# An attention and FFN block on one core: the whole program order placed by a list scheduler, row maxima taken over two PSUM banks at once, and the last 512 queries cut into tiles of 128

## The chip, the cores and the metric

The kernel runs on one core of a Trainium2 chip. Five engines work side by side, each with its own instruction queue: TensorE (PE, matrix products, with PEld for its weight loads), VectorE (DVE), ScalarE (ACT), GpSimd (POOL) and SyncE (SP, which issues DMA transfers here). An engine runs its queue in order and waits on semaphores where it needs another engine's result. Products land in PSUM, which has eight banks of 128 x 512 fp32; the other memory is SBUF. The metric is the device time of the whole program in microseconds (us), the median of several runs.

## The reference

The block is a pre-norm transformer layer over 2048 tokens of width 512, with 32 heads of width 16 and an FFN of width 1792.

```python
qkv = (x @ wqkv).reshape(B, S, 3, H, Dh).transpose(2, 0, 3, 1, 4)   # x here is layernorm(A_x)
scores = einsum("bhqd,bhkd->bhqk", q, k) * (Dh ** -0.5)
o = einsum("bhqk,bhkd->bhqd", softmax(scores, axis=-1), v)
h = x + o.transpose(0, 2, 1, 3).reshape(B, S, D) @ wo
h2 = h + (gelu(ln(h) @ w_gate) * (ln(h) @ w_up)) @ w_down           # gelu in its tanh form
```

Each head has 2048 x 2048 scores. The softmax subtracts the true row maximum, so every score is computed twice: once with queries on the partitions to find the maximum of each row, and once transposed, with keys on the partitions, for the exponential.

## The kernel before

**Tiling.** Tokens are 16 tiles of 128 (`NT`), or 4 chunks of 512 (`NCH`). Four heads make a slot (`NSLOT` = 8), and in a slot each head owns one of four 32-row groups of the PE array. A unit is one chunk of queries and one slot; there are 32.

**First pass, the maxima (p1).** For each unit, `p1_pair` (L518) makes two products at a time, 128 queries against 512 keys of two heads, into two of the banks 0 to 2. `p1_consume` (L527) reduces each bank on DVE to one column of `PM`. After 32 pairs, `negm_pre` (L532 to L541) reduces `PM` to the negated maxima `NEGM` on DVE and splits each into three bf16 parts on POOL. `item_negm` (L548) transposes these parts on PE, ACT copies them to `STG`, and four small DMA transfers (L552) write them as three further rows of `QT`. The keys have ones in those rows (`kbias`), so the second product contains score minus maximum.

**Second pass, the exponentials (p2).** `p2_pair` (L568) makes two products of 128 keys against 512 queries, into two of the banks 3 to 5. `p2_consume` (L578) takes the exponential of each bank on ACT into a ring `PT` of 12 slots. `pv_burst` (L589) multiplies eight of them with the values, four heads side by side by column groups, and accumulates in bank 6 (`PVB`). A column of ones beside the values gives the sum of each row. After 64 of them ACT copies the bank to `OA`; `item_ofin` transposes it (L604), ACT copies it to `OAT`, and POOL divides (L612, L615) into `Otok`.

**The rest.** The projections of Q, K and V (`item_projT`, `item_projV`), and for each finished chunk the output projection, the second layer norm, gate, up and down (`item_onT` to `item_down`), are cut into pieces in one stream, `Dense`. While the two passes run it owns bank 7 alone, and ACT empties it. In the FFN, POOL does the elementwise work of gelu around a tanh on ACT (`gelu_chain`, L729 to L735). When `tail_mode` is set, after the last exponential, ACT uses a gelu of its own and DVE helps.

**What sets the order.** `Plan` records each engine's instructions in the order in which the Python code calls it, and turns the reads and writes given into semaphore waits; nothing is reordered later. The main loop (L817) goes by ticks. A tick has one pair of first-pass products and one pair of second-pass products, in one group:

```python
P.group_begin("pe")
t1 = p1_pair(tick // 32, tick % 32, gp1, signal_last=not p2_ok) if p1_ok else []
t2l = p2_pair(t2 // 32, t2 % 32, 1 - gp1) if p2_ok else []
P.group_end("pe")
```

`group_end` collects all waits of the four products and puts them ahead of the first. The second pass runs 42 ticks behind the first (`P2_START` = 32 + `LAGX`). After the group a tick has a piece of the dense stream, a burst of eight PV products, or up to two `dummy` products (L810), whose results nobody reads. The head before the loop loads x, the QKV weights and wo in six transfers (L294 to L297), normalises all 16 token tiles and transposes them, and makes five projections before the first tick. The three FFN weights (`qkv_finished`) are loaded into the place of the QKV weights once all projections are made.

## Time and profile before

| | us |
|---|---|
| median of 3 runs | 1482.26 (1481.47 to 1482.4) |
| span of the profiled execution | 1477.5 |
| what lies around the profiled span (median less span) | 4.8 |
| busy: PE, DVE, ACT, POOL | 1102.5, 1301.6, 1290.3, 458.3 |
| share of the span: PE, DVE, ACT, POOL | 75%, 88%, 87%, 31% |
| mean granted TensorE clock | 0.991 of full speed |

The span runs from the first to the last instruction; the run's time includes what lies around it. In the profile a row of a group gives the line, the engine, the operation with its tiles (written from read), the shapes, how many there were, their busy time and mean duration (ns), and the idle time ahead of them with the instruction that ended most of it. Busy times of overlapping instructions are counted once, so the busy time of a group can be less than count times mean. Chains of waits and timelines name the same lines. A row of the waits gives who waited for whom, the total, the number of times and the longest. In the view of stretches each engine's busy time is followed by its number of instructions.

### The profile page before, as it was taken

The page shows a single profiled execution, that of the slowest core. Times are in us where ns is not written, and L with a number is a line of the kernel's source. Part 1 is how long each engine was busy: PE and PEld are TensorE (multiplying, and loading weights), DVE is VectorE, ACT ScalarE, POOL GpSimd, SP SyncE. Part 2 cuts the span into 40 slices and gives each one's busy share as a digit, 9 for nine tenths or more (in the row PEclk, how much of TensorE's full clock was granted, in tenths as well). Part 3 has the DMA queues.
Part 4 walks back from the last instruction along what each step waited for, and adds up shares of the span by engine and source line. Part 5 has one row for each costly group of instructions (what it writes and reads, how often), then busy time and mean ns, then how long its engine had stood idle before and what let it go on. Part 6 is the DMA issues. An engine that isn't in the chain of part 4 may idle for free.

```text
span 1477.5 us, 24601 instructions
## 1 busy us (share of the span) xinstructions
PE 1102.5 (75%) x8353; PEld 304.0 (21%) x8494; DVE 1301.6 (88%) x2159; ACT 1290.3 (87%) x2473; POOL 458.3 (31%) x593
## 2 busy tenths in 40 slices
PE   4977777776777777777887777777877777777869
PEld 2311111111112211111222211111222211111224
DVE  5989999998999999999999999999999999998023
ACT  3459999997999999999999999999999999999941
POOL 6000011110112245555212345554112345555130
PEclk9999999998999999999999999999999999999989
DMA  3000000013000000000000000000000000000000
GB/s 114 1 1 2 1 2 2 1 40 112 1 16 1 1 2 2 1 1 2 4 14 14 2 1 2 1 1 1 7 25 1 2 1 2 2 1 2 8 22 16
DMA packets 11531, 15.88 MB, mean 11 GB/s; under 512 B 1040, under 2 KB 9872, under 8 KB 11408
## 3 DMA queue, kind: packets, MB, share of 16 engines
q1 hardware_dynamic: 11408, 14.29, 2.9%
q8 instruction: 71, 1.16, 0.3%
q14 instruction: 52, 0.43, 0.1%
HBM read 11.80 MB, written 2.10 MB: 9 GB/s over the span
## 4 chain that ended last, share of the span: by engine, by line
ACT 32%; DVE 31%; PE 19%; issue 16%; POOL 1%; DMA 1%; SPq 0%; POOLq 0%; ACTq 0%
DVE PM L527 30%; ACT PT L578 27%; PE pbank L518 12%; PE pbank L794 2%; PE pbank L568 1%; PE pbank L462 1%; PE pbank L751 1%; ACT OA L440 1%; PE pbank L770 1%; ACT u_sb L440 1%; DVE stats L315 1%; ACT g_sb L440 1%; ACT sqj L682 0%; ACT OnT L440 0%; ACT QT L440 0%
## 5 line engine op out<-in xcount | busy, mean ns | idle before, releaser
L527 DVE TENSOR_REDUCE PM<-pbank 128x1 f32<-128x512 f32 x2048 | 1258.3, 683 | 70.7 <-PE pbank L568 56.2
L578 ACT ACTIVATE PT<-pbank 128x512 bf16<-128x512 f32 x2048 | 1117.8, 603 | 81.8 <-PE pbank L568 10.3
L518 PE MATMUL pbank<-KT,QT 32*128 32x512 bf16 x2048 | 399.5, 384 | 311.9 <-DVE PM L527 162.3
L568 PE MATMUL pbank<-QT,KT 32*128 32x512 bf16 x2048 | 398.1, 386 | 4.6 <-ACT PT L578 4.3
L518 PEld LDWEIGHTS pbank<-KT,QT 32*128 32x128 bf16 x2048 | 105.0, 91 | 776.3 <-DVE PM L527 767.6
L810 PE MATMUL pbank<-ones_bf,ident 128*128 128x512 bf16 x756 | 239.9, 386 | 5.0 <-ACT PT L578 3.5
L612 POOL TENSOR_TENSOR LINV<-OAT,negone 128x16 f32<-128x16 f32 x32 | 93.2, 2913 | 332.4 <-ACT OAT L440 332.4
L589 PE MATMUL pbank<-PT,VA 128*17 128x512 bf16 x2048 | 156.6, 383 | 0.0
L538 POOL CAST ST<-NEGM 128x16 bf16<-128x16 f32 x32 | 8.1, 252 | 358.1 <-DVE NEGM L532 358.1
L568 PEld LDWEIGHTS pbank<-QT,KT 32*128 32x128 bf16 x2048 | 96.2, 91 | 23.1 <-ACT PT L578 22.6
L729 POOL TENSOR_TENSOR w_sb<-g_sb 128x512 f32<-128x512 f32 x42 | 43.6, 1039 | 136.4 <-ACT g_sb L440 136.4
L810 PEld LDWEIGHTS pbank<-ones_bf,ident 128*128 128x128 bf16 x814 | 52.3, 97 | 110.6 <-ACT PT L578 96.4
L794 PE MATMUL pbank<-wd_sb,GUT 128*128 128x512 bf16 x214 | 57.0, 382 | 3.6 <-issue 1.0
L783 POOL TENSOR_TENSOR GUT<-th_sb,u_sb 128x512 bf16<-128x512 f32 x42 | 53.1, 1265 | 14.3 <-ACT u_sb L440 13.1
L802 DVE CAST out_sb<-pbank 128x512 bf16<-128x512 f32 x5 | 3.5, 692 | 61.2 <-PE pbank L798 61.2
L731 POOL TENSOR_TENSOR w_sb<-w_sb,g_sb 128x512 f32<-128x512 f32 x42 | 53.2, 1267 | 3.5
L735 POOL TENSOR_TENSOR th_sb<-th_sb,g_sb 128x512 f32<-128x512 f32 x42 | 53.2, 1266 | 3.5
L589 PEld LDWEIGHTS pbank<-PT,VA 128*17 128x17 bf16 x2048 | 28.3, 87 | 58.7 <-issue 58.4
L438 ACT ACTIVATE KT<-pbank,kbias 128x512 bf16<-128x512 f32 x32 | 22.1, 689 | 20.0 <-PE pbank L462 20.0
L462 PE MATMUL pbank<-xnT,wk_pad 128*128 128x512 bf16 x122 | 36.6, 415 | 1.9 <-issue 0.6
L462 PE MATMUL pbank<-xnT,wq_pad 128*128 128x512 bf16 x114 | 35.0, 383 | 2.3 <-issue 2.1
L734 POOL TENSOR_SCALAR th_sb<-th_sb 128x512 f32<-128x512 f32 x42 | 25.9, 618 | 28.6 <-ACT th_sb L741 28.6
(120 smaller groups left out, 749.7 us busy)
## 6 DMA issues: line engine op xcount, KB each, us to landing
x_sb<-in_A_x_dram SPq DMA_DIRECT2D x4, 512.0 KB, 5.6
QT<-STG SPq DMA_DIRECT2D x128, 3.0 KB
xres<-in_A_x_dram SPq DMA_DIRECT2D x16, 128.0 KB, 2.2
out_dram<-out_sb SPq DMA_DIRECT2D x16, 128.0 KB, 1.7
wg_sb<-in_B_w_gate_dram SPq DMA_DIRECT2D x1, 1792.0 KB, 7.1
wu_sb<-in_B_w_up_dram SPq DMA_DIRECT2D x1, 1792.0 KB, 11.2
wd_sb<-in_B_w_down_dram SPq DMA_DIRECT2D x1, 1792.0 KB, 16.8
wqkv_sb<-in_A_wqkv_dram SPq DMA_DIRECT2D x1, 1536.0 KB, 10.4
```

Source lines behind the costliest of these rows:

```text
L462: P.op("pe", lambda e, dc=dc: e.matmul(pbank[:, b, :], wp[:, dc, slot, :], xnT[:, dc, 512 * c:512 * c + 512], start=(dc == 0), stop=(dc == ...
L518: P.op("pe", lambda e, g=g, b=b: e.matmul(pbank[:, b, :], QT[32 * g:32 * g + 32, c, slot, 128 * qt:128 * qt + 128], KT[32 * g:32 * g + 32, ...
L527: P.op("dve", lambda e, b=b, qt=qt, kc=kc, g=g: e.tensor_reduce(out=PM[:, par, qt, kc, g:g + 1], in_=pbank[:, b, :], axis=AX.X, op=ALU.max ...
L568: P.op("pe", lambda e, g=g, b=b: e.matmul(pbank[:, b, :], KT[32 * g:32 * g + 32, slot, 128 * kt:128 * kt + 128], QT[32 * g:32 * g + 32, c, ...
L578: P.op("act", lambda e, b=b, pi=pi: e.activation(out=PT[:, pi, :], in_=pbank[:, b, :], func=ACT.Exp), reads=[("pb", b)], writes=[("PT", pi)])
L589: P.op("pe", lambda e, g=g, kt=kt, pi=pi, slot=slot: e.matmul(pbank[32 * g:32 * g + 17, PVB, :], VA[:, kt, 4 * slot + g, :], PT[:, pi, :], ...
L612: P.op("pool", lambda e: e.tensor_tensor(out=li, in0=oat4[:, :, :, 16], in1=negone[:].rearrange("p (q g) -> p q g", g=4), op=ALU.pow), rea ...
L731: P.op(eng, lambda e: e.tensor_tensor(out=ws, in0=ws, in1=gs, op=ALU.mult), reads=[("w", par), ("g", par)], writes=[("w", par)])
L735: P.op(eng, lambda e: e.tensor_tensor(out=ts_, in0=ts_, in1=gs, op=ALU.mult), reads=[("th", par), ("g", par)], writes=[("th", par)])
L783: P.op("pool", lambda e: e.tensor_tensor(out=GUT[:, fc, :], in0=ts_, in1=us, op=ALU.mult), reads=[("th", par), ("u", par)], writes=[("GUT" ...
L794: P.op("pe", lambda e, fc=fc: e.matmul(pbank[:, b, :], GUT[:, fc, 128 * qt:128 * qt + 128], wd_sb[:, fc, :], start=(fc == 0), stop=False), ...
L810: P.op("pe", lambda e: e.matmul(pbank[:, b, :], ident[:], ones_bf[:, 0:512], start=True, stop=True), reads=["ident", "ones_bf"], writes=[( ...
```

## The change

- The tick loop, `Dense`, the deferred calls and the instruction groups are gone. In their place the code that builds the program runs a clock of its own (`Clock`), with an estimated cost and latency for each instruction, and at each step of that clock chooses what PE does next: a fill for the maxima, a fill for the exponentials, a group of PV products, or a piece of a job (projections, transposes, FFN). Work for ACT and DVE is kept as tasks and placed when its inputs are ready by that clock. The chosen order is written into the same `Plan`, and the chip runs it with semaphores as before.
- A fill for the maxima makes two products into banks 0 and 1 or 2 and 3, and one reduction on DVE reads both, 1024 elements to two columns. Exponentials and jobs use banks 4 to 6, all seven when there are no maxima left to make; the PV products accumulate in bank 7.
- The dummy products are left out.
- The head: x comes in five transfers, the QKV weights in three, and projections start when their own token tiles are ready. The first unit takes its keys in the outer loop. Token tiles of chunks 0 and 1 are normalised on DVE, those of 2 and 3 on POOL.
- The last 512 queries are cut by 128-query tile: a unit there is four slots of one tile, and the last unit of all a single slot. The FFN of that chunk is done for tiles 12 to 14 together and for tile 15 alone. There are 34 units.
- Copies out of PSUM that only ACT did may go to DVE when the maxima are more than 48 pairs ahead, or when they are done. `OAT` keeps 17 of 32 columns. The ring `PT` has 16 slots. The place of chunk 3's `h` moves onto that of chunk 0.

The diff, cut to its core:

```diff
-NUNITS = 32
-NPT = 12
-LAGX = 10
-NEGM_DELAY = 4
-PAUSE = 2
-DO_D2 = 1
+INF = float("inf")
+
+NPT = 16
+PVB = 7
+NBANK = 7
...
+    LAT = {"pe": 50, "act": 60, "dve": 60, "pool": 60, "sp": 60}
...
+    def pe(self, mode, pos, n, fn, reads=(), writes=(), sig=False, small=False):
+        dep = self.dep("pe", reads, writes)
+        if self.pe_mode != mode:
+            st = max([dep, self.pe_last] + [e + 100 for e in self.pe_end.values()])
+            self.pe_mode = mode
+            self.pe_end = {}
+        else:
+            st = max(dep, self.pe_last + 4, self.pe_end.get(pos, 0.0))
+        dur = n / 2.4 + 3
+        self.pe_last = st
+        self.pe_end[pos] = st + dur
+        self.P.op("pe", fn, reads=reads, writes=writes, sig=sig)
+        self.note("pe", reads, writes, st + dur + 170)
+        self.free["pe"] = st
+        return st + dur + 170
...
+def act_cost(n, ptr=0, acc=False):
+    return n * 0.8334 + 55 + 93 * ptr + (200 if acc else 0)
...
+def dve_cost(n, rate=1):
+    return n * 1.0417 / rate + 66
...
+        units = [[(c, s_, q_) for q_ in range(4)] for c in range(3) for s_ in range(NSLOT)]
+        for q_ in range(4):
+            for grp in ([0, 1, 2, 3], [4, 5, 6, 7]):
+                if q_ == 3 and grp[0] == 4:
+                    units += [[(3, 4, 3), (3, 5, 3)], [(3, 6, 3)], [(3, 7, 3)]]
+                else:
+                    units.append([(3, s_, q_) for s_ in grp])
         NU = len(units)
...
+        ffn_groups = [list(range(4 * c, 4 * c + 4)) for c in range(3)] + [[12, 13, 14], [15]]
...
+        for (a, b) in ((0, 2), (2, 4)):
+            load(lambda e, a=a, b=b: e.dma_start(out=x_sb[:, a:b, :], in_=xv[:, a:b, :]), ("x", a), [("x", t) for t in range(a, b)], 3400)
+        load(lambda e: e.dma_start(out=x_sb[:, 4:8, :], in_=xv[:, 4:8, :]), ("x", 4), [("x", t) for t in range(4, 8)], 5200)
+        load(lambda e: e.dma_start(out=wqkv_sb[:, :, D:2 * D], in_=wv[:, :, D:2 * D]), "wk", ["wk"], 7000)
+        load(lambda e: e.dma_start(out=x_sb[:, 8:12, :], in_=xv[:, 8:12, :]), ("x", 8), [("x", t) for t in range(8, 12)], 9000)
+        load(lambda e: e.dma_start(out=wqkv_sb[:, :, 0:D], in_=wv[:, :, 0:D]), "wq", ["wq"], 10500)
+        load(lambda e: e.dma_start(out=x_sb[:, 12:16, :], in_=xv[:, 12:16, :]), ("x", 12), [("x", t) for t in range(12, 16)], 12500)
+        load(lambda e: e.dma_start(out=wqkv_sb[:, :, 2 * D:3 * D], in_=wv[:, :, 2 * D:3 * D]), "wv", ["wv"], 14500)
+        load(lambda e: e.dma_start(out=wo_sb[:], in_=A_wo.rearrange("(c p) j -> p c j", p=128)), "wo", ["wo"], 16500)
...
+                if c < 2:
+                    add_task(("dve",), norm, [("x", t), ("rstd", c), ("nmr1", c)], [("xn", t)], 0, 310)
+                else:
+                    norm("pool")
...
+        def p1_list(ui):
+            cs = range(len(units[ui]))
+            if ui == 0:
+                return [(j, kc, gp) for kc in range(4) for j in cs for gp in range(2)]
+            return [(j, kc, gp) for j in cs for kc in range(4) for gp in range(2)]
...
+        def p1_fill(b0, b1):
+            u = st["p1u"]
+            j, kc, gp = p1_lists[u][st["p1i"]]
+            c, slot, qt = units[u][j]
+            par = u % 2
+            for k, b in ((0, b0), (1, b1)):
+                g = 2 * gp + k
+                C.pe("row", g, 512, lambda e, g=g, b=b: e.matmul(pbank[:, b, :], QT[32 * g:32 * g + 32, c, slot, 128 * qt:128 * qt + 128],
+                                                                 KT[32 * g:32 * g + 32, slot, 512 * kc:512 * kc + 512], start=True, stop=True, tile_position=(32 * g, 0)),
+                     [("qT", slot, c), ("aug", c, slot, qt, g), ("kT", slot, kc)], [("pb", b)], sig=(k == 1))
+                bank_free[b] = INF
+            st["p1_out"] += 1
+            last = st["p1i"] + 1 == len(p1_lists[u])
+            def run(eng):
+                fin = C.op("dve", lambda e: e.tensor_reduce(out=PM[:, par, j, kc, 2 * gp:2 * gp + 2], in_=pbank[:, b0:b0 + 2, :], axis=AX.X, op=ALU.max),
+                           [("pb", b0), ("pb", b1)], [("PM", par, j, kc, gp)], dve_cost(1024), dve_lat(1024))
+                bank_free[b0] = bank_free[b1] = fin
+                st["p1_out"] -= 1
+                if last:
+                    negm_pre(u)
+            add_task(("dve",), run, [("pb", b0), ("pb", b1)], [], 2, dve_cost(1024))
...
+            for kl in range(kpb):
+                kt = bi * kpb + kl
+                for ri, (j, slot, qt, m) in enumerate(rr):
+                    col = (kl * n + j) * 128
+                    C.pe("row", g, 128 * m, lambda e, kt=kt, slot=slot, qt=qt, m=m, col=col: e.matmul(
+                        pbank[:, b, col:col + 128 * m], KT[32 * g:32 * g + 32, slot, 128 * kt:128 * kt + 128],
+                        QT[32 * g:32 * g + 32, c, slot, 128 * qt:128 * (qt + m)], start=True, stop=True, tile_position=(32 * g, 0)),
+                        [("qT", slot, c), ("kT", slot, kt // 4)] + [("aug", c, slot, qt + x, g) for x in range(m)], [("pb", b)],
+                        sig=(kl == kpb - 1 and ri == len(rr) - 1), small=(m == 1))
...
+                evac_copy(OAT[:, par, 0:4 * n, :], pbank[:, b, 0:128 * n].rearrange("p (k i) -> p k i", i=32)[:, :, 0:17], [("pb", b)], [("OAT", par)], 68 * n, 0,
+                          then=norm, rel=release(b), engs=("act", "dve"))
...
+        def lead():
+            done1 = sum(len(p1_lists[u]) for u in range(st["p1u"])) + st["p1i"]
+            done2 = sum(len(p1_lists[u]) for u in range(st["p2u"]))
+            if st["p2u"] < NU:
+                done2 += st["p2i"] * len(p1_lists[st["p2u"]]) / p2_len(st["p2u"])
+            return done1 - done2
...
+        def eligible(t, eng):
+            if eng not in t.engs:
+                return False
+            up = getattr(t, "up", None)
+            if up is not None and st["p1_done"]:
+                tail = st["exp_left"] == 0 and st["p2u"] >= NU
+                if eng == "dve":
+                    return "th" in up
+                return not tail
+            if eng == "dve" and len(t.engs) > 1 and not st["p1_done"]:
+                return up is None and lead() > DVE_LEAD
+            return True
...
+        def drained(eng, t0):
+            x = max(C.free[eng], t0)
+            for t in pend:
+                if t.engs[0] == eng and t.prio != 1:
+                    x = max(x, C.dep(eng, t.reads, t.writes)) + t.cost
+            return x
...
+            ok = [bank_free[b] + 57 <= t + 30 for b in range(NBANK)]
+            pairs = [b for b in (0, 2) if ok[b] and ok[b + 1]]
+            only = st["p1_done"] or r1 is None or r1 >= INF
+            pool_s = list(range(NBANK - 1, -1, -1)) if only else [6, 5, 4]
+            singles = [b for b in pool_s if ok[b]]
+            cand = []
+            if r1 is not None and r1 <= t and st["p1_out"] < 2:
+                cand.append((drained("dve", t) - FILL, "p1", min(max(bank_free[b], bank_free[b + 1]) for b in (0, 2)), pairs))
+            if r2 is not None and r2 <= t and st["p2_out"] < 3:
+                cand.append((drained("act", t) - FILL, "p2", min(bank_free[b] for b in pool_s), singles))
+            cand.sort(key=lambda x: x[0])
...
+            for dl, kind, av, have in cand:
+                slack = ROOM_D if kind == "p2" and press else 0.0
+                if have:
+                    join = C.pe_mode == "row" and t < C.pe_last + JOIN and (kind == "p1" or len(singles) > keep)
+                    if dl <= t + AHEAD - slack or join:
+                        go(kind)
+                        return True
...
+            if rv is not None and rv <= t and (room > ROOM_PV or len(pv_groups) > 2):
+                pv_fill()
+                return True
+            if cj is not None:
+                if room > ROOM_D:
+                    cj["segs"].pop(0)()
+                    if not cj["segs"]:
+                        cj["job"].evac(cj["bank"])
+                        jobst["cur"] = None
+                    return True
...
-        def dummy(b, n):
-            for i in range(n):
-                P.op("pe", lambda e: e.matmul(pbank[:, b, :], ident[:], ones_bf[:, 0:512], start=True, stop=True),
-                     reads=["ident", "ones_bf"], writes=[("pb", b)], sig=False)
...
-            P.group_begin("pe")
-            t1 = p1_pair(tick // 32, tick % 32, gp1, signal_last=not p2_ok) if p1_ok else []
-            t2l = p2_pair(t2 // 32, t2 % 32, 1 - gp1) if p2_ok else []
-            P.group_end("pe")
```

## The prediction

> **What bounds the kernel now.** I read first the stretches of the span, cut where its work changes, then the groups of the two busiest engines, then the waits.

> ```profile
> 0.00:34.00 34.00, 13.79 (x85) 8.57 (x86) 17.97 (x48) 13.21 (x22) 22.54 (x33) 1.00 0.36 124
> 34.00:94.00 60.00, 55.48 (x243) 16.66 (x246) 53.50 (x84) 25.63 (x40) 1.00 (x4) 0.94 0.00 1
> 94.00:1363.00 1269.00, 940.37 (x7544) 244.84 (x7669) 1210.57 (x1997) 1188.23 (x2297) 415.63 (x525) 1.00 0.02 8
> ```
> ```profile
> L527 DVE TENSOR_REDUCE PM<-pbank 128x1 f32<-128x512 f32 x2048 | 1258.3, 683 | 70.7 <-PE pbank L568 56.2 <-PE pbank L518 12.9
> L578 ACT ACTIVATE PT<-pbank 128x512 bf16<-128x512 f32 x2048 | 1117.8, 603 | 81.8 <-PE pbank L568 10.3
> L532 DVE TENSOR_REDUCE NEGM<-PM 128x16 f32<-128x64 f32 x32 | 8.5, 264 | 1.1
> ```
> ```profile
> 34.19 26.49 DVE L527 TENSOR_REDUCE PM<-pbank 128x1 f32<-128x512 f32 x41 [7.05 <-PE pbank L518]
> 94.59 2.28 ACT L578 ACTIVATE PT<-pbank 128x512 bf16<-128x512 f32 x4 [0.83 <-PE pbank L568]
> 505.56 3.68 DVE L527 TENSOR_REDUCE PM<-pbank 128x1 f32<-128x512 f32 x6 [0.17 <-PE pbank L568]
> 1362.90 0.27 DVE L532 TENSOR_REDUCE NEGM<-PM 128x16 f32<-128x64 f32 x1
> 1411.96 0.60 ACT L440 ACTIVATE OA<-pbank 128x512 f32<-128x512 f32 x1 [0.47 <-PE pbank L589]
> ```
> The columns of a stretch are start:end, length, then busy time of PE, weight loads, DVE, ACT, POOL, granted clock, DMA share, GB/s. The span splits into a head up to the first maximum (34.2 us), the maxima (34.2 to 1362.9: 1328.7), exps alone (to 1411.5: 48.6) and a tail (66.0). In the long stretch DVE and ACT are both near full: 95% and 94%.

> The floor of DVE: six maxima in 3.68 us, the last lasting 0.683, start (3.68 - 0.683)/5 = 0.599 us apart, 1.198 a pair. Actual: (1328.7 - 32 x 0.2 for the NEGM reductions)/1024 = 1.291 a pair. So 0.093 a pair, 95 us in all, is stall. The first row of groups says where 56.2 of it comes from: a maximum waits for PE at L568, though L568 fills the exps' banks; L518 and L568 stand in one group with all waits ahead of it, so a late exp holds back a free maxima bank.

> **The change, part by part.**

> *Maxima over two banks.* 2048 reductions of 512 become 1024 of 1024. No row shows that size. Upper bound: no saving, 2 x 0.599 = 1.198. Lower: between the 64-element and the 512-element reduction the duration rises (683 - 264)/448 = 0.935 ns an element, so 0.599 + 512 x 0.000935 = 1.078; that slope mixes a source in SBUF with one in PSUM. I take nearly the middle, 1.135: 1024 x 1.135 = 1162 us, 64 less than 1227. DVE is full, so the span moves with it.

> *Order, groups, banks.* The groups go; each fill waits for its own banks, maxima on 0-3, exps and projections on 4-6 (seven once no maxima are left). The 56.2 us of cross-waiting should go; I keep the other 95 - 56 = 39 us (among it the one below: the NEGM rows' transfer queued on SP behind three weight loads, which the new order issues in the same place).

> ```profile
> 339.04 5.36 DMA QT<-STG
> PE pbank L518 <- DMA QT<-STG: 6.2, 1, 6.2
> ```
> What is new is a wait by itself: PE still runs in order, so a fill that waits for DVE stands before the next fill for ACT, and the reverse. The order is fixed from an estimated clock; wherever real times differ, that wait is paid. On SP a NEGM transfer waiting for its copy holds the xres loads and stores behind it, on POOL the next NEGM's split stands behind gate chains, both as now. Bounds for the stall: 0 to the present 95.

> PE's own time, from three spacings: a burst of K=32 products to the next kind takes 500.13 - 499.81 = 0.32; eight PV products 1380.76 - 1380.00 = 0.76 (0.54 for four); three full products 1378.48 - 1377.72 = 0.76, so about 0.22 each and 0.11 for a change of kind.

> ```profile
> 499.81 0.39 PE L518 MATMUL pbank<-KT,QT 32*128 32x512 bf16 x2 [0.26 <-DVE PM L527]
> 500.13 0.34 PE L548 MATMUL pbank<-ident,ST 128*128 128x128 bf16 x3
> 1380.00 0.61 PE L589 MATMUL pbank<-PT,VA 128*17 128x512 bf16 x8
> 1380.76 0.39 PE L568 MATMUL pbank<-QT,KT 32*128 32x512 bf16 x2 [0.15 <-ACT PT L578]
> 1377.72 0.82 PE L794 MATMUL pbank<-wd_sb,GUT 128*128 128x512 bf16 x3
> 1378.48 0.39 PE L568 MATMUL pbank<-QT,KT 32*128 32x512 bf16 x2
> ```
> Now every pair of maxima and its two exp products share one burst. Per pair then: 0.32 + half a PV group of four 0.27 + about 1.06 full products (1088 in all: 320 for Q, K, V, 80 for the output projection, 688 for the FFN) with their changes 0.29 + transposes 0.05 = 0.93. If the exps' products come in a burst of their own: 1.25, more than DVE's 1.135. The new code joins a fill to an open burst where a bank is free, so I take 0.93 to 1.1 and PE not the bound. [...]

> *ACT.* Copies and exps start 0.48 apart (507.25, 507.73), two exps of a pair 0.51; I use 0.49 for exps, 0.48 for the rest.

> ```profile
> 507.25 0.59 ACT L578 ACTIVATE PT<-pbank 128x512 bf16<-128x512 f32 x1
> 507.73 0.60 ACT L440 ACTIVATE g_sb<-pbank 128x512 f32<-128x512 f32 x1
> 508.20 1.11 ACT L578 ACTIVATE PT<-pbank 128x512 bf16<-128x512 f32 x2
> ```
> 2048 x 0.49 = 1003. Others: 332 in the long stretch (2297 less its 1965 exps), plus some 20 projections that now follow the first exp, 6 for two more units, some 35 of the last queries' FFN: 393 x 0.48 = 189. So 1192 us of ACT from its first exp on. The OAT copy of 17 columns in 32 is shorter by half, 34 x 0.2 = 7 us, which I leave out against the accumulating copies that cost more. Copies may go to DVE when the maxima are over 48 pairs ahead.

> *Head.* The loads are smaller and in order of need (nine issues on SP instead of six; the added ones are for late weights, for which nothing waits early). POOL's two clears still hold the first rstd to 9.1, so the first transposes stay at 11.7 and xnT at 14.4. What goes is the wait for the other twelve tiles.

> ```profile
> 5.53 3.51 POOL L309 MEMSET wq_pad<- 128x4096 bf16 x1
> 9.12 0.26 POOL L319 TENSOR_SCALAR rstd<-mv 128x4 f32<-128x4 f32 x1
> 11.71 1.89 PE L331 MATMUL pbank<-ident,xn_sb 128*128 128x128 bf16 x16 [11.71 <-DVE xn_sb L326]
> 12.36 2.06 ACT L333 ACTIVATE xnT<-pbank 128x512 bf16<-128x512 bf16 x4 [10.29 <-PE pbank L331]
> 27.63 4.58 PE L462 MATMUL pbank<-xnT,wk_pad 128*128 128x512 bf16 x15 [0.36 <-PE pbank L331]
> 75.50 0.26 DVE L532 TENSOR_REDUCE NEGM<-PM 128x16 f32<-128x64 f32 x1
> ```
> After 14.4: K of one chunk, four products at 0.43 (half clock, worked out with the clock below), Q the same, copies, first fill: 14.4 + 1.7 + 1.7 + 0.6 + 1.0 = 19.4 instead of 34.2. The stats of chunks 2 and 3 lie in DVE's gap before it. Unit 0's maxima end at 19.4 + 32 x 1.135 = 55.7; POOL's split, transposes, copy and transfer take about 5.8, so the first exp is at 61.5, not 94.6: ACT, the longer of the two, gains 33.

> *Last 512 queries in 128-query tiles.* Two more units; there the exp and PV products are four of 128 columns for one of 512: more PE instructions, no more columns, on PE. The exps alone after the last maximum shrink from 48.6 to one block of 16 exps, 7.8, plus 5.5 of NEGM's way, since the last unit is one slot of 128 queries. Tail: only tile 15 is left. By the present rows 1411.5 to 1426.3 runs one tile's chain in 14.8 us; the shorter power (four columns for sixteen, 1.3 for 2.91) and no foreign products ahead make it 11.4; transposes and copy 1.3; gate and up 112 products of 128 columns at about 0.1, 11.5; last product 1.4; down 15 products 4; copy and store 3; some of tiles 12-14's down 3. Sum 36, from 66.

> ```profile
> 1415.24 2.91 POOL L612 TENSOR_TENSOR LINV<-OAT,negone 128x16 f32<-128x16 f32 x1 [22.88 <-ACT OAT L440]
> 1425.53 0.77 POOL L709 TENSOR_SCALAR OnT<-h_c_72,rstd_100,nmr_101 128x512 bf16<-128x512 bf16 x1
> ```
> ```profile
> L320 POOL TENSOR_TENSOR rstd<-rstd,nhalf 128x4 f32<-128x4 f32 x4 | 5.2, 1298 | 0.3
> ```
> *No dummies.* 756 products less on PE, cover for nothing but the granted clock; below.

> *Sum.* DVE alone: 19.4 + 1162 + 34 x 0.23 (8) + 39 = 1229. ACT alone: 61.5 + 1192 = 1254, plus stall: it idles 1269 - 1188 = 81 now; the same share kept as for DVE (39 of 95) makes 33, so 1287. The difference of 58 is shared: a copy moved costs DVE 0.6 and frees 0.48 of ACT, so 58/2.25 = 26 us move and both end near 1261. With the tail 1297. The profiled span is 1477.5, the median 1482.3, so 4.8 lie around it: 1302, say **1300 us**.

> **The clock, and the rival on the other side.** PE loses cover. Windows of 3.41 us:

> ```profile
> 74.37:77.79 3.42, 0.67 (x6) 0.34 (x6) 1.36 (x3) 0.32 (x2) 1.00 (x4) 1.00 0.00 0
> 77.79:81.20 3.41, 3.28 (x10) 0.77 (x10) 1.45 (x3) 1.04 (x2) 0.00 (x0) 0.50 0.01 3
> 337.20:340.61 3.41, 1.03 (x7) 0.21 (x6) 1.97 (x4) 1.65 (x4) 0.00 (x0) 1.00 1.06 364
> 340.61:344.03 3.42, 0.00 (x0) 0.00 (x0) 0.00 (x0) 0.00 (x0) 0.00 (x0) 0.50 0.83 261
> 487.38:490.80 3.42, 1.81 (x24) 0.75 (x25) 3.16 (x6) 3.32 (x8) 1.76 (x7) 1.00 0.00 0
> 490.80:494.21 3.41, 2.70 (x28) 0.78 (x24) 2.96 (x6) 3.31 (x8) 1.60 (x4) 1.00 0.00 0
> ```
> ```profile
> 94.00:1363.00 1269.00, 231.36 (x729) 50.38 (x783) 1.00 0.02 8
> 77.90 0.61 PE L518 MATMUL pbank<-KT,QT 32*128 32x512 bf16 x2
> 78.57 1.89 PE L462 MATMUL pbank<-xnT,wk_pad 128*128 128x512 bf16 x4
> ```
> PE busy 0.30 of a window was followed by half clock, 0.53 was not; the bound lies between. The first row of the second fence is the dummies alone: without them PE was busy (940 - 231)/1269 = 0.56, and the same work in a shorter span is about 0.6. So I expect full clock, barely covered. [...] *Rival 1, slower:* the clock is granted at 0.50 through the maxima. A burst then takes 0.67 (78.57 - 77.90), a full product (1.89 - 0.6)/3 = 0.43; per pair 0.67 + 0.33 + 0.56 + 0.10 = 1.66 of PE, which becomes the bound: 19.4 + 1700 + 8 + 60 + 5 = about 1790. Against 1.19 a pair, 0.47 x 1024 x share eats the 180 us of gain from a share of 0.37 on: slower than before if more than three eighths of the pairs run so.

> **Other rivals.** *Rival 2:* a reduction over two banks costs as two, 1.198: DVE alone 19.4 + 1227 + 8 + 39 = 1293, + 13 + 36 + 5 = 1347. For it: the fixed part is not seen by itself in any row. Against: 264 ns for 64 elements says there is one. *Rival 3:* bursts are not joined and PE is the bound at 1.25 a pair: 19.4 + 1280 + 8 + 13 + 40 + 5 = 1365. For it: three banks serve exps and projections, so a bank is often not free when a pair's is. Against: the joining code. [...] *Rival 4:* hardly any stall, DVE 1190 and ACT 1254 alone, shared at 1226, tail 32: 1263; with 1.078 a pair 1240.

> **Chances.** Forecast 0.58 (its own range 1270 to 1335), rival 4 0.13, rival 2 0.10, rival 3 0.12, rival 1 and slower in any way 0.06, and 0.01 no change. What a measurement of this kernel tells from no change is about 0.2%, 3 us. Faster 0.93, same 0.01, slower 0.06. The range takes in rival 4 and rivals 2 and 3 with a little above: 1240 to 1375.

> **What would show it.** The maxima group: 1024 reductions, starts 1.135 apart back to back (1.08 to 1.20). First maximum near 19, first exp near 62, last exp near 1261, tail near 36. DVE waiting for PE under 45 us, ACT waiting under 40. Granted clock 1.00 through the maxima. Wrong if the first exp starts by 62 and yet the last is past 1310 with both engines waiting on PE, or if the clock row shows fives.

## The result, and the profile after

The changed kernel takes 1631.73 us (median of four runs, 1628.75 to 1633.89) against 1481.87 for the kernel before on the same chip: a ratio of 1.1014, with a 95% interval of 1.0998 to 1.103. It is slower by 150 us, where the prediction had it faster by 182. The profiled execution has a span of 1632.2 us and a mean granted clock of 0.653, against 0.991 before. From here on a time is the median of all runs of a kernel, while a ratio to the kernel before, run beside it, is that of the fast runs alone, those within 1.5% of the fastest of the same kernel.

From the page of the changed kernel: busy times, the granted clock in forty slices of the span, and the chain that ended last.

```profile
span 1632.2 us, 30475 instructions
...
PE 1496.8 (92%) x10778; PEld 498.1 (31%) x10864; DVE 1269.3 (78%) x1170; ACT 1254.5 (77%) x2434; POOL 378.7 (23%) x519
...
PEclk9965678656576555556655565555655565567999
...
PE 76%; ACT 17%; issue 6%; DVE 1%; DMA 0%; POOL 0%; ACTq 0%; SPq 0%; POOLq 0%
```

PE is busy 394 us longer than before, without the dummies, and it now holds three quarters of the chain that ended last, where it had 19%. The clock row is nines at both ends and fives and sixes between. The stages of the changed kernel (same columns as in the prediction: PE, weight loads, DVE, ACT, POOL, granted clock, DMA share, GB/s) put the loss in one place:

```profile
0.00:28.00 28.00, 10.35 (x72) 6.45 (x74) 17.31 (x44) 9.88 (x17) 24.53 (x37) 0.94 0.48 150
28.00:94.00 66.00, 63.13 (x319) 18.66 (x325) 64.16 (x57) 39.35 (x68) 1.05 (x5) 1.00 0.00 1
94.00:1493.00 1399.00, 1292.04 (x8966) 400.96 (x9025) 1150.38 (x1004) 1122.43 (x2186) 326.35 (x420) 0.60 0.02 7
1493.00:1548.00 55.00, 51.35 (x932) 28.93 (x943) 13.43 (x27) 53.45 (x111) 14.74 (x28) 0.97 0.10 29
1548.00:1632.00 84.00, 79.97 (x510) 43.14 (x508) 24.00 (x42) 29.38 (x56) 12.03 (x32) 1.00 0.04 14
```

From 28 to 94 us the clock is full and DVE is busy 64 of 66 us, as hoped. From there to the last maximum PE runs at a mean of 0.60, and neither DVE (82%) nor ACT (80%) is full any more. The groups and the waits of the changed kernel say what they wait for:

```profile
L616 DVE TENSOR_REDUCE PM<-pbank 128x2 f32<-128x1024 f32 x1024 | 1210.0, 1219 | 255.1 <-PE pbank L609 138.0 <-PE pbank L722 106.5
L732 ACT ACTIVATE PT<-pbank 128x512 bf16<-128x512 f32 x2048 | 1065.9, 616 | 179.4 <-PE pbank L722 143.9 <-PE pbank L609 33.5
L609 PE MATMUL pbank<-KT,QT 32*128 32x512 bf16 x2048 | 624.9, 543 | 3.6 <-DVE PM L616 3.3
```

Ahead of these groups DVE idles 244.5 us for PE (138.0 + 106.5) and ACT 177.4 (143.9 + 33.5), where the prediction had under 45 and under 40. A first-pass product lasts 543 ns in the mean, 384 before. A few rows of the timeline of the changed kernel give the marks (start, length, instruction, idle time before it in brackets):

```profile
11.90 0.56 POOL L497 TENSOR_SCALAR rstd<-mv 128x4 f32<-128x4 f32 x1
...
22.10 1.79 PE L520 MATMUL pbank<-ident,xn_sb 128*128 128x128 bf16 x16 [0.36 <-POOL xn_sb L504]
...
24.11 1.49 PE L557 MATMUL pbank<-xnT,wk_pad 128*128 128x512 bf16 x3 [0.22 <-PE pbank L520]
...
28.03 2.36 DVE L616 TENSOR_REDUCE PM<-pbank 128x2 f32<-128x1024 f32 x2 [6.10 <-PE pbank L609]
...
76.49 0.60 ACT L732 ACTIVATE PT<-pbank 128x512 bf16<-128x512 f32 x1 [0.15 <-PE pbank L609]
...
300.17 2.35 DVE L616 TENSOR_REDUCE PM<-pbank 128x2 f32<-128x1024 f32 x2 [0.18 <-PE pbank L722]
...
1492.19 1.23 DVE L616 TENSOR_REDUCE PM<-pbank 128x2 f32<-128x1024 f32 x1 [0.74 <-PE pbank L722]
...
1546.12 1.73 ACT L732 ACTIVATE PT<-pbank 128x512 bf16<-128x512 f32 x3
```

First maximum at 28.0, first exp at 76.5, last maximum to 1493.4, last exp to 1547.9, end at 1632.2. Two maxima back to back start 2.35 - 1.219 = 1.131 us apart; over the whole pass a pair takes (1493.4 - 28.0)/1024 = 1.431. Sorted by the clock of the 3.41 us window in which they start, from the records of the trace, a pair takes 1.177 us in the 80 windows at full clock and 1.527 in the 327 at half clock (whole windows from 100 us to the last maximum); 733 of the 1024 pairs fall into the latter. That costs 733 x 0.350, some 260 us. It is an estimate: the two kinds of windows need not hold the same work.

The first drop of the clock after the first maximum, in three windows:

```profile
87.13:90.55 3.42, 3.11 (x20) 0.91 (x20) 3.38 (x3) 3.34 (x7) 0.00 (x0) 1.00 0.00 0
90.55:93.96 3.41, 3.10 (x22) 0.85 (x21) 3.41 (x4) 3.41 (x8) 0.00 (x0) 1.00 0.00 0
93.96:97.37 3.41, 3.41 (x15) 0.57 (x14) 2.65 (x4) 2.25 (x5) 0.00 (x0) 0.50 0.00 0
```

PE is busy 3.10 of 3.41 us, 0.91, in the window after which the clock falls. Its gaps are 0.31 us in all, three of about 0.1. DVE and ACT are busy without a break in that window, and in the next they are not.

### The profile page after: what moved, and what is told of

Read it like the earlier page. It is cut to its first block, busy times and chain, and to the rows that moved or that the text cites. A ratio compares the mean times of both kernels' runs of the same rounds, so it can differ in the third digit from the quotient of the medians.

```text
span 1632.2 us, 30475 instructions
## 1 busy us (share of the span) xinstructions
PE 1496.8 (92%) x10778; PEld 498.1 (31%) x10864; DVE 1269.3 (78%) x1170; ACT 1254.5 (77%) x2434; POOL 378.7 (23%) x519
## 4 chain that ended last, share of the span: by engine, by line
PE 76%; ACT 17%; issue 6%; DVE 1%; DMA 0%; POOL 0%; ACTq 0%; SPq 0%; POOLq 0%
PE pbank L722 28%; ACT PT L732 15%; PE pbank L779 14%; PE pbank L609 12%; PE pbank L969 8%; PE pbank L557 5%; PE pbank L1038 3%; PE pbank L801 2%; PE pbank L663 1%; PE pbank L572 1%; PE pbank L877 1%; DVE PM L616 1%; DMA x_sb<-in_A_x_dram 0%; ACT th_sb L991 0%; DVE stats L487 0%
## 5 line engine op out<-in xcount | busy, mean ns | idle before, releaser
L616 DVE TENSOR_REDUCE PM<-pbank 128x2 f32<-128x1024 f32 x1024 | 1210.0, 1219 | 255.1 <-PE pbank L609 138.0
L732 ACT ACTIVATE PT<-pbank 128x512 bf16<-128x512 f32 x2048 | 1065.9, 616 | 179.4 <-PE pbank L722 143.9
L722 PE MATMUL pbank<-QT,KT 32*128 32x128 bf16 (+1 forms) x3584 | 807.0, 392 | 78.8 <-ACT PT L732 54.9
L609 PE MATMUL pbank<-KT,QT 32*128 32x512 bf16 x2048 | 624.9, 543 | 3.6 <-DVE PM L616 3.3
L722 PEld LDWEIGHTS pbank<-QT,KT 32*128 32x128 bf16 x3584 | 244.1, 107 | 567.4 <-ACT PT L732 486.9
L779 PE MATMUL pbank<-PT,VA 128*17 128x128 bf16 (+1 forms) x3584 | 288.1, 397 | 0.0
L808 POOL TENSOR_TENSOR LINV<-OAT,negone 128x16 f32<-128x16 f32 (+2 forms) x34 | 94.1, 2767 | 330.6 <-ACT OAT L431 303.0
L779 PEld LDWEIGHTS pbank<-PT,VA 128*17 128x17 bf16 x3584 | 76.8, 100 | 179.3 <-issue 168.0
L969 PE MATMUL pbank<-hnT_c,wu_sb 128*128 128x512 bf16 (+2 forms) x264 | 74.4, 397 | 6.0 <-ACT PT L732 2.5
L969 PE MATMUL pbank<-hnT_c,wg_sb 128*128 128x512 bf16 (+2 forms) x262 | 69.8, 385 | 6.2 <-ACT PT L732 1.2
## 6 DMA issues: line engine op xcount, KB each, us to landing
wu_sb<-in_B_w_up_dram SPq DMA_DIRECT2D x1, 1792.0 KB, 11.4
```

The source lines that it names most:

```text
L609: C.pe("row", g, 512, lambda e, g=g, b=b: e.matmul(pbank[:, b, :], QT[32 * g:32 * g + 32, c, slot, 128 * qt:128 * qt + 128], KT[32 * g:32 ...
L616: fin = C.op("dve", lambda e: e.tensor_reduce(out=PM[:, par, j, kc, 2 * gp:2 * gp + 2], in_=pbank[:, b0:b0 + 2, :], axis=AX.X, op=ALU.max) ...
L722: C.pe("row", g, 128 * m, lambda e, kt=kt, slot=slot, qt=qt, m=m, col=col: e.matmul(pbank[:, b, col:col + 128 * m], KT[32 * g:32 * g + 32, ...
L732: fin = C.op("act", lambda e: e.activation(out=PT[:, s0, :], in_=pbank[:, b, :], func=ACT.Exp), [("pb", b)], [("PT", s0)], act_cost(512), ...
L779: fin = C.pe("col", g, 128 * m, lambda e, g=g, kt=kt, j=j, slot=slot, m=m, col=col, ri=ri: e.matmul(pbank[32 * g:32 * g + 17, PVB, 128 * j ...
L808: pool(lambda e: e.tensor_tensor(out=LINV[:, par, 0:4 * n], in0=oat4[:, :, 16], in1=negone[:, 0:4 * n], op=ALU.pow), [("OAT", par), "negon ...
```

## The experiments

The theory to test: the clock of PE falls because the dummies are gone, and with it goes the time. The rival: the new order itself (PE bound, fills in the wrong order) costs the time, and the clock is a by-product. Then, once that was decided: which measure of PE's work goes with the clock in these runs?

### The kernel before without its dummies

```diff
 def dummy(b, n):
-    for i in range(n):
+    for i in range(0):
```

> The kernel before with its 756 dummy products left out and nothing else changed. Theory A (the granted clock follows the share of the array's cells at work in a window of 3.41 us, rows times columns, and holds above about 0.28 of full speed): in stretches without projections or FFN a tick then has 4 x 512 columns on a quarter of the array and 2 x 512 on 17 of 128 columns, 648 full-array cycles in 1.29 us or 0.21: the clock falls to a mean of 0.55 to 0.75 and the time rises to 1550 to 1650. Theory C (the clock is a by-product, the loss is in the new order): the clock may fall, but the time stays within 2% of 1482, since DVE and ACT still set the pace.

Measured: 1599.29 us, ratio 1.079 (1.0761 to 1.0818), clock 0.731. From its page:

```profile
span 1596.7 us, 23016 instructions
...
PEclk9997777765556677777686677777687677777699
...
L527 DVE TENSOR_REDUCE PM<-pbank 128x1 f32<-128x512 f32 x2048 | 1296.2, 685 | 145.8 <-PE pbank L568 108.4
...
L518 PE MATMUL pbank<-KT,QT 32*128 32x512 bf16 x2048 | 518.4, 500 | 403.2 <-DVE PM L527 272.2
```

Nothing else was touched, and the old order loses 118 us by it, with the same falling clock and DVE idle for PE again. (8494 against 7680 weight loads: the dummies were 814; the 756 of the prediction are those that left a record.) So with the dummies the clock of this order is 0.991 and without them 0.731, and their removal alone costs an order that is otherwise fast 118 of the 150 us by which the changed kernel is slower. That speaks for the clock as the main cause of the loss. Whether the new order would be as fast as forecast at full clock is not decided by it. Theory A's range came true, but not for its reason: its count by cells does not hold up below.

### Dummies put back where the new order has room

A record of what PE was given in the last 3.4 us of the planned clock (`activity`), and a dummy in a free bank when that is low and neither DVE nor ACT is due soon. The second has the same order with dummies of 17 columns.

```diff
+        TH = 0.4
+        ROOM_F = 250.0
...
+            free_b = [b for b in range(NBANK) if ok[b]]
+            if free_b and room > ROOM_F and started() and C.activity(t) < TH:
+                dummy(free_b[-1])
+                return True
```

> The kernel after, to which a full-array dummy product of 512 columns is added (into a free bank, when nothing is due within 0.25 us) wherever the planned share of array cells at work over the last 3.41 us is under 0.40; 332 of them. Theories A and B (B: the clock follows the time in which PE streams anything): clock 0.95 or more, time 1290 to 1360, maxima 1.13 to 1.20 apart. Theory C: clock up, time still over 1480.

> As e2, the same program order and the same number of dummy products of 512 columns, but each with 17 of the 128 array columns only, so PE streams as long and an eighth of the cells work. Theory A: the clock stays under 0.75 and the time is 1580 or more. Theory B: clock 0.95 or more and the time of e2.

Then with the level at 0.45, a room of 100 ns, and PV products counted a quarter:

> The kernel after with 280 full-array dummy products of 512 columns, put where nothing is due within 0.1 us and the planned share of the array at work is under 0.45 (a K=32 or a 17-column product counted as a quarter of the array). Also, as in the next three, an up job waits for the same buffers as its gate job. Theory A, now with the bound read from the windows of the runs so far (full clock kept above about 0.35 of the array): the plan leaves one window in eight under 0.35, and one is enough to lose the clock, so the clock is mixed, 0.70 to 0.90, and the time 1420 to 1560. Theory C (the order loses the time whatever the clock): over 1480 at any clock.

Measured: 1754.93 us (clock 0.656), 1742.39 (0.67) and 1700.76 (0.658; ratio 1.1468, 1.1417 to 1.152). All are slower than without, and each missed its Theory A. The first two leave out a wait that all later runs have (an up job waits for the same buffers as its gate job), so what they compute is not the layer; only their times and clocks are read here. The planned clock places `n / 2.4 + 3` ns for a product, 216 ns for 512 columns, as full products start 0.216 us apart at full clock in the trace of the changed kernel, and finds its room there. At half clock they start 0.40 to 0.43 us apart in that trace, so the planned room was not there. The clock stayed where it was without these dummies (0.653). My reading was that the level has to be held in every window and not on average; these three runs do not show it.

### Dummies forced ahead of the fills

```diff
+            if free_a and started() and (C.pe_mode != "row" or t >= C.pe_last + 60) and C.activity(t) < 0.37:
+                dummy(free_a[0] if len(pairs) == 0 else free_a[-1])
+                return True
```

> As the run before with 530 dummy products, now put wherever the planned share falls under 0.37 even if a fill is due; the plan leaves one window in 24 under 0.35. Theory A: clock 0.90 or more, time 1390 to 1450, below the kernel before. Theory C: over 1480 at a clock of 0.90 or more.

> The order and the number of dummy products of the run before, but each product uses 17 of the 128 array columns, so PE streams as long while a quarter of the array's tiles work. Theory A: clock under 0.75, time 1600 or more. Theory B (the clock follows the time in which PE streams anything): clock and time of the run before.

> 661 dummy products, put wherever the planned share falls under 0.40; the plan leaves one window in 60 under 0.35. Theory A: clock 0.95 or more, time 1400 to 1440, not much better than with 530 since each further product costs PE time. Theory C: over 1480.

Measured: at 0.37, 1812.97 us (clock 0.687) with full dummies and 1772.84 (0.708) with 17 columns; at 0.40, 1635.65 (0.845; ratio 1.0947, 1.0907 to 1.0987). Theory A's clocks and times, 1390 to 1450 and 1400 to 1440 us, were missed by far. With full dummies a planned level 0.03 higher came with a clock of 0.845 instead of 0.687. In the last of them the maxima end at 1434 instead of 1493, but the forced dummies took the places of FFN pieces: FFN products worth 452 full ones come after the last maximum, against 379 in the changed kernel, and 189 us of the span are left there. The 17-column dummies held the clock no worse than the full ones (0.708 against 0.687), which speaks against a count of the cells at work.

### Work paced instead of dummies added

FFN pieces and projections are held back while the level is above `PACE`, and pulled ahead, with a dummy only where no piece is ready, when it is below `KEEP`:

```diff
+            if started() and (...) and C.activity(t) < KEEP:
+                if job_piece(t, singles, False):
+                    return True
+                ...
+                    dummy(free_a[-1])
```

> The kernel after, with the projections and the FFN spread: their pieces start only while the planned share of the array over the last 3.41 us is under 0.50, and where it falls under 0.40 the next piece, or if none is ready a full-array dummy product, goes ahead of the fills; 377 dummies. Unlike the runs with 280 to 661 dummies, none takes the place of a piece of real work. The plan leaves 5 windows of 366 under 0.35. Theory A (share of the array, full clock kept above about 0.37, taken back above about 0.31): clock 0.90 or more, maxima 1.17 to 1.25 apart, tail under 90 us, time 1340 to 1420. Theory C (the order loses the time whatever the clock): over 1480.

> As the run before with a bound of 0.44 in place of 0.40 and dummies up to 0.50; 571 dummies, one window of 372 under 0.35. Theory A: clock 0.97 or more, time 1350 to 1420. Theory C: over 1480.

> The order of the run before, its 571 dummies on 17 of the 128 columns instead of all: PE streams as long, a quarter of the array's tiles work. Theory A: the clock falls, under 0.80, time over 1500. Theory B (the clock follows the time in which PE streams anything): clock and time of the run before.

Measured: at 0.40, 1585.84 us (ratio 1.0602, 1.0534 to 1.067); at 0.44, 1485.79 (1.0014, 0.9986 to 1.0043), and with 17 columns 1489.46 (1.0032, 0.999 to 1.0075). Single executions at 0.44 differ, 1473.8 to 1537.8 us at clocks of 0.956 to 0.898. The 150 us are back, by work on PE that nobody reads and by a more even order of work that was there; how much each gives isn't told apart. Theory A's times, 1340 to 1420 and 1350 to 1420 us, were missed again, and Theory C's mark, over 1480, was met: at a clock of about 0.95 this order is as fast as the old one, not faster. The thin dummies held the clock as the full ones did (0.938 to 0.958 in five executions), against Theory A of the last run. Its page:

```profile
span 1487.7 us, 31242 instructions
...
PEclk9999999858999999998558999999999999989999
```

Two long stretches at half clock are left (288 to 346 us, 694 to 790 us). In them a pair takes 1.87 us, outside 1.23.

### Dummies of 64 rows and of 17 columns

The kernel before, with nothing changed but the shape of its dummies: 64 rows of the array in place of 128, then 17 columns in place of 128.

```diff
-                P.op("pe", lambda e: e.matmul(pbank[:, b, :], ident[:], ones_bf[:, 0:512], start=True, stop=True),
+                P.op("pe", lambda e: e.matmul(pbank[:, b, :], ident[0:64, :], ones_bf[0:64, 0:512], start=True, stop=True),
```
```diff
-                P.op("pe", lambda e: e.matmul(pbank[:, b, :], ident[:], ones_bf[:, 0:512], start=True, stop=True),
+                P.op("pe", lambda e: e.matmul(pbank[0:17, b, :], ident[:, 0:17], ones_bf[:, 0:512], start=True, stop=True, tile_position=(0, 0)),
```

> The kernel before with its dummy products made of 64 rows of the array in place of 128; columns, moving length, number and place are unchanged. What is open is what the grant counts: the rows of the array that are fed, or only the time for which products stream. Rows: over the pass of the maxima the kernel before feeds 0.48 of the rows of a window (real products 0.25, dummies 0.23); with half the rows the dummies give 0.115 and the window 0.37, which is about the level below which windows lost the clock in the runs so far: many drops, clock 0.75 to 0.92, 1500 to 1570 us. Time: a dummy streams as long as before, so nothing changes: clock 0.99, 1481 us within 4.

> The kernel before with its dummy products made of 17 columns of the array in place of 128; rows, moving length, number and place are unchanged. Rows alone count: clock 0.98 to 0.99 and 1481 us within 5, as before. Rows times columns (the cells of the array at work) count: the dummies give 0.03 in place of 0.23 of a window, and the run goes as the one without dummies went, clock 0.73 to 0.77 and 1570 to 1600 us.

Measured: 1551.15 us (ratio 1.0472, 1.0448 to 1.0495; clock 0.869) with 64 rows, 1479.35 (0.9994, 0.9985 to 1.0003; clock 0.990) with 17 columns. From the page of the first, then of the second:

```profile
PEclk9998999985558799998898699999897679998779
...
L810 PE MATMUL pbank<-ones_bf,ident 64*128 64x512 bf16 x814 | 305.5, 445 | 0.2
```
```profile
PEclk9999999999999999999999999999999999999979
...
L810 PE MATMUL pbank<-ones_bf,ident 128*17 128x512 bf16 x814 | 257.4, 383 | 0.9
```

The same number of products, at the same places, with the same moving length. With 87% of the columns taken away the time and the clock stay (1479.35 us against 1481.06, 0.990); with half of the rows taken away 70 us are lost and the clock is 0.869. To compare, I added up for each 3.41 us window between 100 us and the last maximum what the records show. (The clock records of the traces change only on a grid of 3.413 us.) Cells are rows times columns of the array that hold weights. By rows, a product counts its columns streamed times the share of the 128 rows that it feeds (K=32 a quarter, 64 rows a half); of the PV products four start within some 10 ns and the next four 0.22 us after them in the trace of the kernel before, so each counts a quarter. With full products 0.216 us apart at full clock, some sixteen fill a window. Means over the windows at full clock:

| kernel before, dummies of | time PE streams | cells at work | rows fed | clock | us |
|---|---|---|---|---|---|
| 128 x 128 | 0.50 | 0.45 | 0.48 | 0.991 | 1482 |
| 128 rows x 17 columns | 0.52 | 0.35 | 0.51 | 0.990 | 1479 |
| 64 rows x 128 columns | 0.52 | 0.41 | 0.45 | 0.869 | 1551 |
| none | 0.39 | 0.34 | 0.38 | 0.731 | 1599 |

Only the rows stand in the order of the clock (0.991 and 0.990 being the same). The expectation's 0.23 for the dummies held the FFN and the projections too; the dummies alone are 0.13, so half of their rows leaves 0.51 - 0.065, or 0.45, and not 0.37. (The first row is some 0.02 low, for the records that are missing.) All sixteen traces together, 3517 windows at full clock:

| rows fed in the window | windows | followed by half clock |
|---|---|---|
| under 0.32 | 177 | 155 |
| 0.32 to 0.39 | 535 | 175 |
| 0.39 and more | 2805 | 2 |

The counts move by a few with how a product across a border is shared out. Other measures sort the same windows worse: of some 330 drops, the best single bound on the rows fed misjudges 165 windows, on the time PE streams 273, on the cells at work 326.

And back: of 2809 windows at half clock, with the same count in time (full products start 0.40 to 0.43 us apart there, against 0.216), 10 of 1180 under 0.55 were followed by full clock, 61 of 61 above 0.80. The changed kernel at half clock lies at a mean of 0.52 in the windows that stayed and 0.70 in those that came back, and holds 0.4 products of 512 columns on the full array, from projections and the FFN, in a mean window of the former and 3.2 in one of the latter: the drops of that trace ended with richer windows.

### Held above that level

The paced order with 17-column dummies again, at 0.48 (764 dummies), and at 0.44 with the level kept over 2.4 us instead of 3.4, so that single windows lie closer to the mean (556 dummies):

```diff
-        KEEP = 0.44
+        KEEP = 0.48
```
```diff
-        lo = t - 3413.0
+        lo = t - 2400.0
```

> The paced order of the changed kernel with 17-column dummies, held at a planned share of 0.48 in place of 0.44 (764 dummies in place of 571). In the run at 0.44 each drop began with a window of 0.36 or 0.37 and 49 windows of the maxima ran at half clock, 1.87 us a pair against 1.23. If the grant follows the rows fed, the higher level takes most of these drops away: clock 0.97 or more, a pair 1.23 to 1.26, 1440 to 1475 us, faster than before. If it follows something else (bursts, chunk starts), the clock stays about 0.94 and the added products cost time: 1490 to 1520 us.

> The paced order at a planned share of 0.44, but the share is kept over stretches of 2.4 us in place of 3.4 us (556 dummies of 17 columns), so that single windows lie closer to the mean. If drops come from the low windows of an uneven order, there are fewer of them for the same number of dummies: clock 0.96 to 0.99, 1440 to 1475 us. If the mean share sets it, the clock stays 0.93 to 0.95 and the time 1475 to 1495 us.

Measured: 1493.61 us (ratio 1.0076, 1.005 to 1.0103) and **1457.54 us (0.9847, 0.9832 to 0.9863)**. The first holds the clock at 0.98 to 0.99 in five of six executions and still loses: its pairs take 1.26 us at full clock, against 1.23. Neither side of its expectation was right, as the clock rose and the products cost what it gave. The second is the first to take less time than the kernel before, 1.5% less, with an interval clear of 1. Its page:

```profile
span 1458.6 us, 31289 instructions
...
PE 1369.0 (94%) x11420; PEld 477.3 (33%) x11420; DVE 1242.5 (85%) x1161; ACT 1265.1 (87%) x2463; POOL 486.7 (33%) x635
...
PEclk9999997899999999999967999999999999999999
...
L624 DVE TENSOR_REDUCE PM<-pbank 128x2 f32<-128x1024 f32 x1024 | 1191.2, 1218 | 89.7 <-PE pbank L730 42.4
L740 ACT ACTIVATE PT<-pbank 128x512 bf16<-128x512 f32 x2048 | 1085.2, 616 | 98.9 <-PE pbank L730 56.1
```

The clock is 0.972 in this execution, DVE waits 90 us before its maxima where it waited 255, the last maximum starts at 1313.7 and the last exp ends at 1410.6. Its mean of rows fed is hardly higher than in the 0.44 run before it (0.47 against 0.46, over windows at full clock), but 4 of 331 of these windows lie under 0.37 where 13 of 314 did (40 of 80 in the changed kernel). That fits the first reading in its expectation, in which the drops come from the low windows.

## Why the prediction was wrong

**The step that failed** is the one on the dummies: "cover for nothing but the granted clock" and then "I expect full clock, barely covered". It rested on two windows, PE busy 0.30 with a drop and 0.53 without, and on a mean of 0.56 to 0.6 without dummies. Busy PE did not tell the drops from the rest: the window ahead of the first drop was 0.91 busy by the profile, whose ends of products are modelled, and 0.57 by the time in which columns stream, above the mean of 0.50 at which the kernel before has a clock of 0.991. In rows fed it was 0.33. The same count was in reach: without dummies a pair has four first- and second-pass products at a quarter and half a group of four PV products at a quarter, 4 x 0.25 + 2 x 0.25 = 1.5 full products, and about 1 of FFN and projections where they come evenly. 2.5 products of 0.216 us in 1.18 us are 0.46, but in stretches without them 1.5 give 0.27, and all 40 drops in the trace of the changed kernel between 100 us and the last maximum follow windows under 0.39, 25 of them windows under 0.32. A mean over the pass hid that.

**Rival 1** named this effect and its place, though not what sets it off, with the chance 0.06. Its price of 1.66 us a pair was measured as 1.53, against 1.18 instead of 1.19 at full clock; its point of balance, three eighths of the pairs, was passed at three quarters. "Wrong if the clock row shows fives" was the mark that came true.

**Of 335 us between the forecast's span (1297) and the measured one (1632)**, 287 lie up to the last exp (1261 against 1547.9) and 48 in the tail (36 against 84). Of the 287, 9 are the head, 237 the pass of the maxima and 41 the exps behind the last maximum. The half clock's 260, counted from 1.177 us a pair where the forecast has 1.20, cover the pass.

**Right:** the reduction over two banks, 1.131 us against 1.135; its bounds held, and rival 2 (1.198) falls. In the 80 windows at full clock PE is near the forecast: a pair in 1.18 with PE busy 0.91 of the time is 1.07 of PE, so rival 3's 1.25 did not come there.

**Half right, the stall.** 39 us of DVE's waiting were to stay. At half clock this can't be judged; in the best paced order, at 0.972, DVE still waits 90 us. Its dummies are part of that, and how much isn't told apart. Separate banks did not do away with waiting for the other engine's fills: PE runs one queue, and 42.4 of these us are still put down to the exps' products (L730).

**The exps behind the last maximum** are a miss of their own. The forecast had 16, and 13 us with the way of NEGM. In the changed kernel 103 exps start after the last maximum does and take until 54.5 us after its end, in the best paced order 161 and 96 us. The maxima run ahead of the exps by some 45 pairs at 100 us; later that is 50 in the changed kernel, and 80 in the best paced order, where the kernel before keeps 42. So a small last unit did not shorten this stretch. What lets the exps fall behind isn't told apart.

**What the clock does not explain.** The best paced order, at 0.972, takes 1457.5 us, 155 more than the forecast; its last exp ends at 1410.6 and not at 1261. PE is busy 94% of the span there and holds 66% of the chain that ended last, so "PE not the bound" did not hold either. The dummies are 201.2 us of PE's busy time there. No run has the new order at full clock without them, so the 1300 us were neither reached nor ruled out.

**The head** gave 28.0 instead of 19.4. POOL's first `rstd` came at 11.9 and not at 9.1, since its clears of `ST` and `VA` now stand ahead of it; I counted two clears of four. Then PE's queue has a V projection and the transposes of later chunks, which wait for POOL (22.10), ahead of K (24.11). I had put K right behind its own inputs and did not look at what the planner had put ahead of it. The first exp followed at 76.5 instead of 61.5.

**The tail.** The forecast had tile 15 alone left after the last exp. The groups of the changed kernel from 1547.9 us on:

```profile
L1038 PE MATMUL pbank<-wd_sb,GUT 128*128 128x512 bf16 x110 | 25.1, 379 | 0.3 <-PE pbank L969 0.3
L969 PE MATMUL pbank<-hnT_c,wu_sb 128*128 128x512 bf16 x55 | 14.3, 379 | 0.1
L969 PE MATMUL pbank<-hnT_c,wg_sb 128*128 128x512 bf16 x54 | 14.1, 379 | 0.1
L969 PE MATMUL pbank<-hnT_c,wg_sb 128*128 128x384 bf16 x56 | 11.4, 326 | 0.0
L969 PE MATMUL pbank<-hnT_c,wu_sb 128*128 128x384 bf16 x56 | 11.4, 326 | 0.0
L969 PE MATMUL pbank<-hnT_c,wu_sb 128*128 128x128 bf16 x56 | 3.8, 219 | 0.0
L969 PE MATMUL pbank<-hnT_c,wg_sb 128*128 128x128 bf16 x56 | 3.8, 219 | 0.6 <-DVE hnT_c L434 0.6
```

Nearly all of chunk 2's gate and up (109 of 112 products of 512 columns), all of tiles 12 to 14's and eight tiles' down are still there: 51 us of gate and up beside tile 15's own, and 25 of down, tile 15's among them. The clock is 1.00 in this stretch and the order is fixed when the program is built, so this is a miss of its own: the FFN was placed late, and I had assumed that it was placed where PE had room.

## What to carry to other kernels

Before a product that nobody reads is taken out, ask what it does for the clock, and work that out for the leanest windows and not for the mean: here, with small row tiles, PE was busy 0.91 of a window by the profile and the clock was 0.50 in the next. What gave the most in this case was to spread the full-array work that there is over the windows, with a thin product over all rows in the gaps, and not more of them than needed: 1457.54 us with 556 of them and the level kept over 2.4 us, against 1481.06 for the kernel before and 1493.61 with 764. The order was planned at full speed, and the plan held only as long as the clock did: a pair took 1.18 us at full clock and 1.53 at half.
